# K in channel halves, bf16 masks, and dh's product on two engines, in a training step of a state-space layer with a gated feed-forward

## The chip, the core and the metric

The kernel runs on one core of one Trainium2 chip. The core has TensorE for matrix products (they land in PSUM), VectorE, ScalarE and GpSimd for elementwise work, and SyncE, which here only issues DMAs; ScalarE and GpSimd issue DMAs too. Each engine carries out its own instructions in order and waits for the others by semaphores. In the profile's rows the engines are called PE, PEld (TensorE's weight loads), DVE (VectorE), ACT (ScalarE), POOL (GpSimd) and SP (SyncE); a q behind the name is the engine's queue of DMA issues. The metric is the device time of one execution in microseconds (us).

## The reference

The layer is `out = x + s * g` on x of 2048 positions by 512 channels (bf16), and the kernel returns it together with the gradients for the eleven inputs of which it is a function, given `grad_out`. With xn the layer norm of x:

```python
# s: diagonal state-space layer (512 channels, 128 states), as a causal convolution
P = exp(dt*A[:, :, None] * arange(L));  K = einsum("dn,dnl,dn->dl", C, P, dt*B).real
y = irfft(rfft(pad(xn)) * rfft(pad(K)))[:L];  s = y + xn * Dskip
# g: feed-forward with silu on both sides, 1792 hidden units
h = silu(xn @ w1);  g = silu(h @ w2)
out = x + s * g
# _out, _vjp = jax.vjp(f, A_u, A_re, A_im, B_re, B_im, C_re, C_im, log_dt, Dskip, w1, w2); return out, *_vjp(grad_out)
```

Positions l are rounded to bf16 in the reference (`arange(L)` is cast to the type of A), so beyond 256 several lags share one value of K: 656 rows of K (some of them padding) stand for the 2048 lags.

## The kernel before

**Tiling.** Positions lie on the 128 partitions, 16 to a partition; so a tile of x, xn, DS or DO is 128 x 16 x 512 in bf16. The convolution is done as a Fourier transformation in two steps: a product with a 128-point table (TF, TI) over the partitions and 16-point products (Wf, Vi) with a 32 x 32 transposition on VectorE between them (`turn`, the STREAM_TRANSPOSE rows). It runs for one half H of the channels at a time, 256 of 512. `fwd_first` is the first step (eight groups, each evicted from PSUM into FA), `fwd_second` the second; `inv_first` and `inv_mm` are the way back. `cplx_mul` multiplies two spectra on VectorE.

**Stages.** Stage 1 (to about 158 us) computes the layer norm, the feed-forward forward pass, the powers of the state-space eigenvalues and, in `gen_masks`, small constants, among them MK, a mask with the lag values (float32). Stage 2 makes K: for four chunks of channels, `chunk_tables` builds tables X and CY on VectorE, `chunk_K` multiplies them into Kout (four steps for a chunk, called k in the score; chunk b and half u of it hold channels 32b + 16u to 32b + 16u + 15 of each of four blocks of 128), and `gen_xt` transposes X, collects it in XT (four buffers) and stores it (t). The spectra of xn (u) run beside it, then those of DS (f), the gradient that reaches y. At the end of the stage `store_K` writes all of Kout to the DRAM tile Kud; `load_K`, early in stage 3, reads it back as K_b with the rows repeated for the 2048 lags, by 17 DMAs on the queues of SP, ScalarE and GpSimd. `K_b` takes the place that DO_all has later.

Stage 3 transforms K (a, b: `forward` for half 0 and 1), multiplies spectra (p, e; and d, `chain`, for the gradient of K), goes back for y (x) and for the gradient of xn (z), turns each result into output: S_s and DO_all (y, `YOut.out`, after `YOut.sil` and `YOut.pre`, s), DXC (c), dK (v). `sums` (g) adds the lags that share a row of K and stores them in dKgd; `early` (t of the third score) loads them into Gt.

Stage 5 holds four things beside each other: the gradient of w2 (w, `Dw2`), the slabs of the state-space gradients (l, `Slabs`: `Gb` spreads Gt by the mask MK into Gbd, `P2` multiplies Gbd with XTl, `D3` and `P3` finish; y is `gen_y`, the other operand), the gradient of h (h, `Bwd.dh`), and after it the gradients of xn (x, `Bwd.dx`), of w1 (m) and the final output (z, `Out0`). A step of `dh` takes two tiles of 128 hidden units for 512 positions, computes silu' on ScalarE (sd), multiplies on TensorE into PSUM (ps_da), multiplies both on VectorE into dhT (line 1740), and turns the step before, through dhk, into DRAM (dhd).

**Order.** The order of the work is written out by hand as strings, the scores: `play` takes one letter after the other and runs the next piece of the generator with that name. A capital letter lets the piece evict PSUM on VectorE (`ev`, line 77, and `evs`), a small one on ScalarE. Pieces that only issue a DMA can be held (`hold`, `flush`) until the next piece of their kind. Nothing else orders the work: each engine and each DMA queue takes what it was given, in that order.

```python
nc.vector.tensor_tensor(out=self.dhT[:, f0:f0 + 2, :], in0=ps[:], in1=sd[:], op=ALU.mult)   # dh
MK = const.tile([P, 2, 16, 2], F32, name="MK")                                              # gen_masks
```

Of the kernel before, what the change touches and what calls it, by code (L numbers as in the profile page):

```python
# [138 lines left out]

def fwd_first(k, A, src, H):  # L140

    nc = k.nc
    d = slice(HW * H, HW * H + HW)
    for q in range(8):
        ps = k.pd.tile([P, 2, 2, HW], F32, name="ps_f", tag="pd")
        for j in range(2):
            for c in range(2):
                nc.tensor.matmul(out=ps[:, j, c], lhsT=k.TF[:, 2 * q + j, c, :], rhs=src(2 * q + j)[:, d], start=True, stop=True)
# [68 lines left out]
def kernel(ctx, tc, A_u, A_A_re, A_A_im, A_B_re, A_B_im, A_C_re, A_C_im, A_log_dt, A_Dskip, B_x, B_w1, B_w2, grad_out,  # L217
# [50 lines left out]
def gen_masks(k):  # L268
# [656 lines left out]
def chunk_K(k, b, t):  # L925
# [4 lines left out]
    for u in range(2):  # L930
# [1021 lines left out]
```

## Time and profile before

| what | us |
|---|---|
| median of 3 runs (679.77 to 685.35) | 682.53 |
| profiled execution | 682.6 |
| its span, first to last instruction | 680.8 |
| TensorE busy | 571.8 |
| VectorE busy | 570.1 |
| ScalarE busy | 453.6 |
| GpSimd busy | 96.0 |

The page gives an engine's busy time, its share of the span and its instructions; a matmul's end is modelled, and products overlap, so a busy TensorE is not one at its peak. The mean granted TensorE clock was 0.953. In rows of groups, `out<-in` are the program's names, then the shape, the count, the busy time in us and the mean of one in ns, and behind the second bar the idle time ahead of them with what ended it. In rows of waits stand the waiting engine, tile and line, what it waited for, the total in us, the number of waits and the longest. In rows by stretch stand its ends and length, then busy time and instruction count of PE, PEld, DVE, ACT and POOL, the granted clock, the share of the DMA engines and GB/s.

### The profile page before, as it was taken

The page shows a single profiled execution, that of the slowest core. Times are in us where ns is not written, and L with a number is a line of the kernel's source. Part 1 is how long each engine was busy: PE and PEld are TensorE (multiplying, and loading weights), DVE is VectorE, ACT ScalarE, POOL GpSimd, SP SyncE. Part 2 cuts the span into 40 slices and gives each one's busy share as a digit, 9 for nine tenths or more (in the row PEclk, how much of TensorE's full clock was granted, in tenths as well). Part 3 has the DMA queues.
Part 4 walks back from the last instruction along what each step waited for, and adds up shares of the span by engine and source line. Part 5 has one row for each costly group of instructions (what it writes and reads, how often), then busy time and mean ns, then how long its engine had stood idle before and what let it go on. Part 6 is the DMA issues. An engine that isn't in the chain of part 4 may idle for free. (4 is left out here: it accounts for less than half of the span.)

```text
span 680.8 us, 14322 instructions
## 1 busy us (share of the span) xinstructions
PE 571.8 (84%) x5668; PEld 339.3 (50%) x5668; DVE 570.1 (84%) x940; ACT 453.6 (67%) x551; POOL 96.0 (14%) x170
## 2 busy tenths in 40 slices
PE   2798877886777787779897869799998898999997
PEld 1344333334666576557675645355544544544553
DVE  5899978859899847888989997968998997879655
ACT  4799988967689955898979943465546645343341
POOL 1121100020100314211212251122201000000000
PEclk9989988977798997899999979799999999999999
DMA  8756568573899879965467879879978948986976
GB/s 252 233 182 222 198 219 283 195 241 146 248 278 300 257 199 258 324 224 166 134 194 238 201 196 255 232 187 257 254 204 209 250 135 254 266 245 196 315 228 204
DMA packets 173622, 154.58 MB, mean 227 GB/s; under 512 B 70574, under 2 KB 141750, under 8 KB 173556
## 3 DMA queue, kind: packets, MB, share of 16 engines
q1 hardware_dynamic: 157428, 112.70, 57.5%
q0 software_dynamic: 11920, 38.08, 17.3%
q10 hardware_dynamic: 4208, 2.89, 1.5%
q8 instruction: 44, 0.72, 0.4%
q14 instruction: 22, 0.18, 0.1%
HBM read 76.81 MB, written 67.65 MB: 212 GB/s over the span
## 5 line engine op out<-in xcount | busy, mean ns | idle before, releaser
L723 PE MATMUL ps_h<-XNT,W 128*128 128x512 bf16 x224 | 59.7, 418 | 20.7 <-ACT hs L77 14.4
L696 PE MATMUL ps_o<-W,aT 128*128 128x512 bf16 x224 | 55.3, 397 | 3.1 <-ACT aT L725 3.1
L1739 PE MATMUL ps_da<-DOT,W2T 128*128 128x512 bf16 x224 | 52.8, 379 | 1.1 <-DMA dhd<-dhk 0.9
L1568 PE MATMUL ps_w<-DO_all,KXW 128*128 128x512 bf16 x224 | 53.2, 391 | 0.0
L1801 PE MATMUL ps_dx<-KXW,dhT 128*128 128x512 bf16 x224 | 51.3, 379 | 1.4 <-DVE dhk L77 1.4
L723 PEld LDWEIGHTS <-W 128*128 128x128 bf16 x224 | 23.3, 105 | 52.8 <-issue 31.6
L1901 PE MATMUL ps_w<-dhc,xn 128*128 128x448 bf16 x256 | 49.2, 353 | 0.0
L77 ACT CAST FZ<-ps_i 128x1024 bf16<-128x1024 f32 x44 | 43.1, 1034 | 4.6 <-PE ps_i L187 4.6
L77 ACT CAST FA<-ps_f 128x1024 bf16<-128x1024 f32 x39 | 38.4, 1048 | 10.4 <-PE pt_xt L1012 7.4
L1740 DVE TENSOR_TENSOR dhT<-ps_da,sd 128x1024 bf16<-128x1024 f32 x28 | 34.1, 1221 | 13.2 <-ACT sd L213 12.3
L173 PE MATMUL ps_s<-FA,Wf 128*64 128x256 bf16 x384 | 35.0, 318 | 10.9 <-ACT FX L77 6.8
L1810 ACT ACTIVATE dxn<-dxn,c,rstd 128x512 f32<-128x512 f32 x16 | 13.0, 814 | 44.2 <-DVE c L1809 44.2
L696 PEld LDWEIGHTS <-aT 128*128 128x128 bf16 x224 | 22.7, 102 | 33.0 <-issue 5.3
L77 ACT CAST Vb<-ps_V 128x1024 bf16<-128x1024 f32 x26 | 26.0, 1016 | 19.1 <-PE ps_V L1637 14.7
L77 ACT COPY dhk<-pt_dh 128x1024 bf16<-128x1024 bf16 x20 | 20.1, 1007 | 27.0 <-DMA dhd<-dhk 17.8
L77 ACT COPY XT<-pt_xt 128x1024 bf16<-128x1024 bf16 (+1 forms) x35 | 32.5, 967 | 8.1 <-PE pt_xt L1012 3.1
L1901 PEld LDWEIGHTS <-xn 128*128 128x128 bf16 x256 | 25.0, 98 | 23.7
L187 PEld LDWEIGHTS <-Vi 64*128 64x128 bf16 x576 | 27.4, 95 | 16.9 <-issue 6.5
L1568 PEld LDWEIGHTS <-KXW 128*128 128x128 bf16 x224 | 21.4, 100 | 26.7 <-issue 5.4
L1360 PE MATMUL ps_v<-FZ,TI 128*128 128x256 bf16 x192 | 25.2, 282 | 10.9 <-DVE FZ L162 8.5
L1801 PEld LDWEIGHTS <-dhT 128*128 128x128 bf16 x224 | 21.3, 98 | 25.4 <-issue 2.3
L1739 PEld LDWEIGHTS <-W2T 128*128 128x128 bf16 x224 | 21.2, 98 | 25.3 <-issue 2.2
(313 smaller groups left out, 1457.1 us busy)
## 6 DMA issues: line engine op xcount, KB each, us to landing
XTd<-XT SPq DMA_DIRECT2D x20, 512.0 KB, 4.6
XP<-UXd POOLq DMA_DIRECT2D x16, 512.0 KB, 4.9
XTl<-XTd SPq DMA_DIRECT2D x31, 256.0 KB, 4.8
hTd<-hs SPq DMA_DIRECT2D x28, 256.0 KB, 3.4
aTd<-aT SPq DMA_DIRECT2D x28, 256.0 KB, 2.8
dhc<-dhd SPq DMA_DIRECT2D x16, 448.0 KB, 6.1
XYd<-XYg SPq DMA_DIRECT2D x25, 256.0 KB, 3.8
hsb<-hTd SPq DMA_DIRECT2D x18, 256.0 KB, 3.1
```

Of the source, the lines that this page charges most:

```text
L77: (k.nc.vector.tensor_copy if k.by_dve else k.nc.scalar.copy)(out=out, in_=in_)
L173: nc.tensor.matmul(out=ps[64 * h:64 * h + 64, c, j], lhsT=k.Wf[:, c, 0:64], rhs=A[:, 2 * (v + j) + h], start=True, stop=True)
L187: nc.tensor.matmul(out=ps[:, h, j], lhsT=Vc[z], rhs=y[z, c, v % 4 + j, :], start=(n == 0), stop=(n == len(Y) - 1))
L696: nc.tensor.matmul(out=pso[:], lhsT=aT[:, ft, tt * P:(tt + 1) * P], rhs=W2[:, ft, :], start=(ft == 0), stop=(ft == FT - 1))
L723: nc.tensor.matmul(out=ps[:, j], lhsT=W1[:, dk, ft * P:(ft + 1) * P], rhs=XNT[:, dk], start=(dk == 0), stop=(dk == DK - 1))
L1360: k.nc.tensor.matmul(out=ps[:, j], lhsT=k.TI[:, t0 + j, c, :], rhs=Z[:, 2 * (t0 + j) + c], start=(c == 0), stop=(c == 1))
L1568: nc.tensor.matmul(out=ps[:], lhsT=A[:, t, :], rhs=k.DO[:, t, :], start=(t == 0), stop=(t == T - 1))
L1739: nc.tensor.matmul(out=ps[:, j], lhsT=self.W2T[:, ft // 2, dk, j * P:(j + 1) * P], rhs=self.DOT[tc_][:, dk], start=(dk == 0), stop=(dk == ...
L1740: nc.vector.tensor_tensor(out=self.dhT[:, f0:f0 + 2, :], in0=ps[:], in1=sd[:], op=ALU.mult)
L1801: nc.tensor.matmul(out=psx[:], lhsT=dhT[:, ft, t % 4 * P:(t % 4 + 1) * P], rhs=self.W1T[:, ft, :], start=(ft == 0), stop=(ft == FT - 1))
L1810: nc.scalar.activation(out=dxn[:], in_=dxn[:], func=ACT.Identity, scale=k.rstd[:, t:t + 1], bias=c12[:, 0:1])
L1901: nc.tensor.matmul(out=ps[:], lhsT=k.xn[:, t, dk * P:(dk + 1) * P], rhs=ch[i][:, t, :], start=(t == 0), stop=(t == T - 1))
```

## The change

- **Halves.** H no longer means the lower or upper 256 channels but every second block of 64 (`half`): half 0 holds the channels 128x to 128x + 63, which are complete when chunks 0 and 1 of K are done. `store_K` writes one half after chunk 1 and one after chunk 3, from within `chunk_K`, to a DRAM tile of its own; `load_K` reads one half, called by a new part h (`taps`), once in stage 2 and once in stage 3; and half 0's first transformation, a, may begin in the second score of stage 3. K_b's halves lie in `dkp`, a pool now opened in stage 2, and in the place of DO. XT gets three buffers instead of four.
- **Layout behind it.** xn, DS, DO and DXC are now read or written in blocks of 64 channels. `YOut` loads co and cG as two full rows of 512 channels for a partition, multiplies them into DO_all early (`pre`), and `out` multiplies the convolution into DO_all in place. dKgd is split by halves, and Gt is loaded by 20 DMAs instead of 6. Out0's first product is made for each position by itself, into g.
- **Masks.** MK is bf16 and holds each value twice, and Gbd is laid out so that the innermost step of every operand is one element. The weights of `P2` are then 32 columns with a step of 16 elements.
- **dh.** ScalarE copies ps_da to dhT as bf16, and VectorE multiplies that in place with sd.
- **Places.** T12 of the slabs and two of the last stage's big tiles lie in `dkp`.
- **Orders.** All scores are new.

```diff
-SCORE_1 = "pppppppppppppggpgpppGppgppppgppppgppppppgppppppgppgppgpppgppppggppppppppgppppgpMpgpppGpgpppppppgpgppppggpmpmmppppgppppgpppppgpppppppppgmgppmmpMgggGmmgttGmgmggmmmgGgggGmttGgt"
+SCORE_1 = "ppppppppppppppppggggGpgpppppgpppgppppgpgppppppppppgppppppgppppgpgppppgppppggpppppMGpppgppppgpppppggpppppGpppmgmpppgppgpppppggpgpppppmpgpppgmGgpmpGgmMmmggpgmGgmmmtggttGtGmmtg"
 SCORE_2 = (
-    "guTuuuuuuuuwttTtgUtKttkkgctgtttkggtotgtuuuttkTtgucttgktgtkgtkto",
-    "uT",
-    "uuuuutuKkuguuwukwtkctwgUugwuuggtutuutTuKtKTKk",
-    "ttT",
+    "",
+    "uuguwuwuttuTTtTKugkuttkttcktuougggugugut",
+    "ttuutuuttTgcktkkgtgtutkgotuuuttguwhuuKUtkcgtggtttuuguutktktuutwwUtt",
+    "KKTKk",
 )
 SCORE_3 = (
-    "Tt",
-    "UFqFqFqkFFFffttqftfffqFnknuffDffffkfUfTuUDfffddFdn",
-    "kaaFadafdafdndkfdkDsdFdfaffafBvvDvAbbvidaddskbkgsabgagaFgdddGddDapijDpabdasadaixbxbvevjxtvvzjxtisgzpBjigpxgeggxtxzeizesxzzjbzzijiXfzbbyybbsepbpbsycsbxxcxpyxxpzxgsxxzejxezcljzqsylsesssyzyzzslYZZCsCCCC",
+    "TTu",
+    "ffffnfffqfAhafqaaqakTqfkfFfffuqnfFTDUuUffffTkffffdadnadFdtfddFkfdkfd",
+    "dFkdfDffbbabdbvDvkvvddjgaadagnddgFsdaegiddkGifaabDqiddbaabppabdxitxvtxjvpxvxvBxzzejzbgipjsessxzexiXzigszsggsgistbbpbbpbszzpbjgsszybxysxjspsjxexxjeexxexxssylyzczzzzzzzZylycccyclcCCY",
 )
 SCORE_5 = (
-    "wuuuyuuwlWWywwhYlwLYllYylywylyllwwullwlhhwlhlwL",
-    "YLlHlWwYulyLhylwhyllwlwwYhwLyYYLwwlhylwlwyWLHwwlWloYlhHlolLhyloLoooloyhllYxlllLhxLlxlxxlx",
-    "xzxxHzhhzxxhhxHfHxfxxxhxHxhxthftHtthxxxhzxxxfhxtmtttzfftfxxftmtmtMxftmmfffxMxxttfftfzmMfzzfmffmrtrrmrzz",
+    "luwWhuhLyWuwwywuyyLwywHwLlhYulWlwLlyuhlWlwulylHlw",
+    "yYYLhYLyLwlHWywlHlWlwYWwLllyWYHwllylwWHlwlLwwHoollylloyloLhyylolYoloHlllhLLyxLxLllxxxl",
+    "xzxxHxhzhxxHhfxfHthxxxxHxhxxfHHHtthxxtxxfhzxxhxtxtxtfMfffttmtfmtxtmfMftfMztffMfxtzxfxtmzmMmzrzffftzrrzmr",
 )
+def half(x, H):
+    return x.rearrange("p (x h r) -> p x h r", h=2, r=64)[:, :, H] if len(x.shape) == 2 else x.rearrange("p t (x h r) -> p t x h r", h=2, r=64)[:, :, :, H]
...
-                nc.tensor.matmul(out=ps[:, j, c], lhsT=k.TF[:, 2 * q + j, c, :], rhs=src(2 * q + j)[:, d], start=True, stop=True)
+                nc.tensor.matmul(out=by64(ps[:, j, c]), lhsT=k.TF[:, 2 * q + j, c, :], rhs=src(2 * q + j, H), start=True, stop=True)
...
-    MK = const.tile([P, 2, 16, 2], F32, name="MK")
+    MK = const.tile([P, 2, 16, 2, 2], BF16, name="MK")
...
+        if end and u:
+            store_K(k, b // 2)
         yield
-def store_K(k):
+def store_K(k, H):
     for e in range(2):
         for s in range(2):
             z = 32 * (2 * e + s) + e
-            d0 = 256 * e + 128 * s
-            (k.nc.scalar if s else k.nc.sync).dma_start(k.Kud[:, d0:d0 + 128].rearrange("(h l) d -> l h d", l=16), k.Kout[z:z + 32 - e:2])
+            d0 = 128 * e + 64 * s
+            (k.nc.scalar if s else k.nc.sync).dma_start(k.Kud[H][:, d0:d0 + 64].rearrange("(h l) d -> l h d", l=16), k.Kout[z:z + 32 - e:2, :, 64 * H:64 * H + 64])
...
-            XT = xs.tile([P, 8, 2, P], BF16, name="XT", tag="XT", bufs=4)
+            XT = xs.tile([P, 8, 2, P], BF16, name="XT", tag="XT", bufs=3)
...
+    def taps():
+        K_b = k.K_b = [k.dkp.tile([P, T, HW], BF16, name="K_b", tag="dK")]
+        for H in range(2):
+            if H:
+                K_b.append(k.do.tile([P, T, D], BF16, name="K_b", tag="DO")[:].rearrange("p t d -> p (t d)")[:, 0:T * HW].rearrange("p (t d) -> p t d", d=HW))
+            load_K(k, K_b, H)
+            yield
...
         for H in range(2):
-            d = slice(HW * H, HW * H + HW)
-            g = k.dKgd[0:640, d].rearrange("(h l) d -> h l d", l=16)
-            nc.sync.dma_start(Gt[2 * H::4], g[0:32])
-            nc.sync.dma_start(Gt[1 + 4 * H:62 + 4 * H:8], g[32:40])
-            nc.sync.dma_start(Gt[65 + 4 * H:66 + 4 * H, 0, :], k.dKgd[640:641, d])
+            for e in range(2):
+                g = k.dKgd[H][0:640, 128 * e:128 * e + 128].rearrange("(h l) (s r) -> h l s r", l=16, s=2)
+                for s in range(2):
+                    nc.sync.dma_start(Gv[2 * e::4, :, s, H], g[0:32, :, s])
+                    nc.sync.dma_start(Gv[1 + 4 * e:62 + 4 * e:8, :, s, H], g[32:40, :, s])
+                nc.sync.dma_start(Gv[65 + 4 * e:66 + 4 * e, 0, :, H], k.dKgd[H][640:641, 128 * e:128 * e + 128].rearrange("a (s r) -> a s r", s=2))
...
-            r[nm] = k.y2.tile([P, 4, HW], BF16, name=nm, tag=nm, bufs=3)
-            q.dma_start(r[nm][:], piece(src, n))
+            r[nm] = k.y2.tile([P, 2, D], BF16, name=nm, tag=nm, bufs=3)
+            q.dma_start(r[nm][:], src[:, 2 * n:2 * n + 2, :])
...
-        TT(out=S[:], in0=S[:], in1=g[:], op=ALU.mult)
-        TT(out=S[:], in0=S[:], in1=x[:], op=ALU.add)
+        for t in range(TS):
+            gx = g[:, t].rearrange("p (x h r) -> p x h r", h=2, r=64)
+            TT(out=gx, in0=S[:, t].rearrange("p (h x r) -> p x h r", h=2, r=64), in1=gx, op=ALU.mult)
+        TT(out=g[:], in0=g[:], in1=x[:], op=ALU.add)
...
-        self.G[i] = self.sw.tile([P, 16, 2, 16, 2], BF16, name="Gbd", tag="Gbd", bufs=2)
+        self.G[i] = self.sw.tile([P, 2, 16, 2, 8, 2], BF16, name="Gbd", tag="Gbd", bufs=2)
...
+        src = k.Gt[:, :, c0:c0 + 16].unsqueeze(2).to_broadcast([P, 16, 2, 16])
         for g2 in range(2):
-            nc.vector.tensor_tensor(out=G[:, :, g2], in0=k.Gt[:, :, c0:c0 + 16].rearrange("p l g -> p g l").unsqueeze(3).to_broadcast([P, 16, 16, 2]),
-                                    in1=k.MK[:, g2].unsqueeze(1).to_broadcast([P, 16, 16, 2]), op=ALU.mult)
+            nc.vector.tensor_tensor(out=G[:, g2].rearrange("p l e n m -> p l e (n m)"), in0=src, in1=k.MK[:, g2].rearrange("p l e m -> p (l e) m").unsqueeze(2).to_broadcast([P, 32, 8, 2]), op=ALU.mult)
...
-        nc.vector.tensor_tensor(out=self.dhT[:, f0:f0 + 2, :], in0=ps[:], in1=sd[:], op=ALU.mult)
+        d = self.dhT[:, f0:f0 + 2, :]
+        nc.scalar.copy(out=d, in_=ps[:])
+        nc.vector.tensor_tensor(out=d, in0=d, in1=sd[:], op=ALU.mult)
```

More of the change, by code (lines that the diff above doesn't have):

```diff
@@ L922, in chunk_tables, with chunk_K @@
     yield
-def chunk_K(k, b, t):
+def chunk_K(k, b, t, end):
     nc = k.nc
@@ L1235, in forward @@
             yield
+    play(k, SCORE_3[0], **parts)
+    drain(k, parts, "w")
+    banks(k, 3, 1)
+    assert k.turned >= 33
+    lo.close("w2s", "xc", "ko", "sa", "mm")
+    ro.close("cyb")
+    k.do = lo.open("do"); k.mm = lo.open("mm", 3); k.fa = lo.open("fa", 2)
+    k.ux = lo.open("ux", 6)
+    k.sel = lo.open("sel")
+    k.row = k.sel.tile([DK, P], BF16, name="row")
+    sels = []
+    FA, W1 = (k.fa, "FA"), (k.tfp, "W1")
+    parts.update(a=forward(0, *FA), q=skip(), n=gsum_sel(k, k.sel, sels), k=loads(Uk, k.UXd), d=chain())
+    play(k, SCORE_3[1], **parts)
+    drain(k, parts, "tu")
+    ro.close("sb", "xs", "uw")
+    k.kxw = ro.open("kx").tile([P, 8192], BF16, name="KXW", tag="KX")
+    dkp = k.dkp
+    k.y2 = ro.open("y2", 2)
+    y = k.y = YOut(k)
+    for n in range(3):
+        y.load(n)
     def products(Y, U, conj):
@@ L1257, in gates @@
             yield
+            if n == 0:
+                assert got.count(0) and got.count(1)
+                k.DO = k.do.tile([P, T, D], BF16, name="DO_all", tag="DO")
             y.pre(n)
```

123 lines of the change are left out of this document (51 added, 72 removed).

## The prediction

> **What bounds the kernel now.** I read the page's busy times first, then busy time by stage, then the waits of the stages that leave most room, then the groups that the change touches.
>
> ```profile
> span 680.8 us, 14322 instructions
> PE 571.8 (84%) x5668; PEld 339.3 (50%) x5668; DVE 570.1 (84%) x940; ACT 453.6 (67%) x551; POOL 96.0 (14%) x170
> PE 17%; DMA 9%; DVE 8%; ACT 3%; issue 2%; SPq 1%; DVEq 0%; ACTq 0%
> 407.76 9.19 DMA XYy<-XYd
> ```
>
> No engine is full over the span, and the chain that ended last has no owner: followed back it reaches only to 407.76 us, and of these 40% of the span TensorE holds 17, DMA 9 and VectorE 8. So the room must be looked for stage by stage. The next rows give, after the stretch and its length, the busy time of TensorE, its weight loads, VectorE, ScalarE and GpSimd.
>
> ```profile
> 158.00:246.00 88.00, 65.05 (x1478) 52.16 (x1481) 78.50 (x132) 72.06 (x84) 11.61 (x20) 0.90 0.79 239
> 246.00:300.00 54.00, 41.92 (x535) 32.88 (x524) 40.87 (x52) 38.99 (x43) 14.19 (x30) 0.91 0.90 263
> 300.00:396.00 96.00, 85.29 (x1070) 64.03 (x1070) 91.35 (x74) 86.01 (x92) 20.09 (x32) 1.00 0.64 185
> 396.00:420.00 24.00, 17.98 (x124) 10.31 (x123) 18.64 (x21) 5.37 (x7) 9.92 (x15) 0.86 0.90 241
> 448.00:520.00 72.00, 70.17 (x696) 37.69 (x698) 61.94 (x87) 40.43 (x47) 12.98 (x25) 1.00 0.86 226
> 420.00:620.00 200.00, 185.69 (x1639) 97.29 (x1637) 171.90 (x275) 105.74 (x119) 22.43 (x42) 0.98 0.83 223
> ```
>
> Two stretches are badly filled: 246 to 300 us, where the busiest engine works 41.92 of 54 us, and 396 to 420 us, where it works 18.64 of 24. Between them VectorE is the bound (91.35 of 96, 95%). Behind them TensorE is (185.69 of 200, 93%; 97% between 448 and 520), with VectorE at 86% and ScalarE at 53%. The change touches all four.
>
> **Part A, K by halves.** Here is the hole it aims at, as waits between 246 and 300 us and as the accesses to K.
>
> ```profile
> ACT FA L77 <- PE pt_xt L1012: 7.4, 1, 7.4
> DVE XT L77 <- ACT Kout L77: 4.2, 1, 4.2
> DVE FX L77 <- PE ps_s L173: 2.6, 3, 1.9
> PE pt_xt L1012 <- ACT XT L77: 3.3, 1, 3.3
> L956 ACTq DMA_DIRECT2D Kud<-Kout x2: 663/676/690, 248.1 to 248.8; - x2
> L956 SPq DMA_DIRECT2D Kud<-Kout x2: 712/1100/1489, 249.1 to 249.9; - x2
> L977 ACTq DMA_DIRECT2D K_b<-Kud x1: 348/348/348, 257.1 to 257.1; - x1
> L980 ACTq DMA_DIRECT2D K_b<-Kud x1: 1265/1265/1265, 257.5 to 257.5; - x1
> L983 ACTq DMA_DIRECT2D K_b<-Kud x1: 1341/1341/1341, 258.8 to 258.8; - x1
> L148 PE MATMUL ps_f<-K_b,TF x64: 269/273/284, 284.7 to 334.7; 128*128 128x256 bf16 x64
> ```
>
> K is stored at 248 to 250 us and its loads are issued from 257.1 on: they follow the stores' landing. ScalarE issues three of them, and it is in order: its evictions stand behind DMA issues that cannot go yet, which is the idle 7.4 us, whatever name the wait carries. K is first read at 284.7, so K itself is not waited for; what is lost is the blocked queue, and the fact that only the spectrum of DS and the lag chain are there to interleave, each a series of product, eviction and transposition. After the change, half 0 is stored with the eighth of 16 steps of K, and eleven score entries lie between that and its loads; half 1 has fourteen between store and load. The block should go, and one whole forward transformation of K (eight evictions, one turn) becomes filler for this stretch. Were it filled as well as the stretch behind it, it would take 41.92 / 0.95 = 44 us: at most 10 gained. Of the other side: two more stores and three more loads are issued by ScalarE, 2 x 0.676 + 0.348 + 1.265 + 1.341 = 4.3 us if none is covered. I take -6, nearer to the full hole, since the filler is real work that stands at 284 to 300 us today. **A: -6, between -10 and +4.3.**
>
> The layout goes with it and I cost it at nothing: products, evictions and the DO multiplications keep count and size, with runs of 64 elements in them. If the 16 multiplications of DO lost their pace through that and ran like the 1213 ns rows below rather than at 684, it would be 16 x 0.53 = 8.5 us on VectorE; the rows show no such pattern, so this stays as an upper end.
>
> ```profile
> L1326 SPq DMA_DIRECT2D Gt<-dKgd x2: 546/572/599, 336.8 to 353.5; - x2
> L1327 SPq DMA_DIRECT2D Gt<-dKgd x2: 601/620/639, 337.5 to 354.1; - x2
> L1328 SPq DMA_DIRECT2D Gt<-dKgd x2: 383/394/406, 338.2 to 354.8; - x2
> L1624 DVE TENSOR_TENSOR Gbd<-Gt,MK 128x512 bf16<-128x512 bf16 x32 | 20.4, 682 | 0.0
> DMA packets 173622, 154.58 MB, mean 227 GB/s; under 512 B 70574, under 2 KB 141750, under 8 KB 173556
> q1 hardware_dynamic: 157428, 112.70, 57.5%
> ```
>
> Gt's loads become 20 instead of 6, on SP: at these durations 2 x (4 x 0.57 + 4 x 0.62 + 2 x 0.39) = 11 us of SP's queue instead of 3. Gt is loaded by 355 us and first read by L1624 after 411 us, so some 50 us cover it. Pieces shrink: counted from the access patterns, K's stores go from 256 to 128 bytes (4 x 16 x 41 = 2,624 pieces become 5,248), K's loads from some 1,024 pieces of 2 KB to 2,048 of 1 KB, Gt's from 2 x (32 x 16 + 8 x 16 + 1) = 1,282 of 512 bytes to 5,128 of 128; against that, co and cG are read in runs of 2 KB instead of 512 bytes, 16 x 128 x 4 = 8,192 pieces becoming 2,048. The net is some 1,350 packets on 173,622. By the q1 row a packet takes 0.575 x 16 x 680.8 us / 157,428 = 40 ns of one engine, so the 6,470 added pieces of 128 bytes are 16 us of all sixteen engines, spread over 100 us.
>
> [...] No row here separates the rate of a 128-byte piece from that of a 512-byte one.
>
> **Part B, the seam at 396 to 420 us.**
>
> ```profile
> PE ps_v L1360 <- DVE FZ L162: 6.0, 1, 6.0
> ACT Y L1035 <- DMA XYy<-XYd: 18.6, 1, 18.6
> ```
>
> TensorE waits 6.0 us for the last transposition, with nothing but products of its result ahead in the order; ScalarE waits 18.6 us for a load. In the new order the last turn of x (Z) is followed by outputs of y, a step of l and evictions that do not need it, and stage 5 plays h, dh's first steps, at its fifth entry instead of its fifteenth. The 6.0 is the ceiling, zero the floor, if SP or GpSimd deliver XTl no sooner. **B: -3.**
>
> **Part C, fewer evictions on VectorE in stage 3.** Capital letters evict on VectorE: F falls from 11 to 6, D from 6 to 4, C from 5 to 2.
>
> ```profile
> L77 DVE CAST FA<-ps_f 128x1024 bf16<-128x1024 f32 x9 | 10.5, 1213 | 0.4 <-PE ps_f L148 0.4
> L77 ACT CAST FA<-ps_f 128x1024 bf16<-128x1024 f32 x39 | 38.4, 1048 | 10.4 <-PE pt_xt L1012 7.4 <-PE ps_f L148 2.9
> ```
>
> Ten go: 12.1 us off VectorE, 10.5 onto ScalarE. From 300 to 396 the two hold 91.35 and 86.01; level, at 88.7 and the same 95%, the stretch would take 93 instead of 96. **C: -2, between -3 and 0.**
>
> **Part D, stage 5.**
>
> ```profile
> L1740 DVE TENSOR_TENSOR dhT<-ps_da,sd 128x1024 bf16<-128x1024 f32 x28 | 34.1, 1221 | 13.2 <-ACT sd L213 12.3 <-PE ps_da L1739 0.7
> L1462 DVE TENSOR_TENSOR zS<-zS,zg 128x1024 bf16<-128x1024 bf16 x8 | 5.5, 684 | 9.3 <-DMA zg<-gd 9.3
> L901 DVE TENSOR_TENSOR m<-X 128x512 bf16<-128x512 bf16 x4 | 1.7, 414 | 0.0
> L213 ACT ACTIVATE sd<-hsb 128x1024 bf16<-128x1024 bf16 x28 | 29.3, 1057 | 0.0
> L77 ACT COPY dhk<-pt_dh 128x1024 bf16<-128x1024 bf16 x20 | 20.1, 1007 | 27.0 <-DMA dhd<-dhk 17.8 <-PE pt_dh L1755 7.3 <-issue 1.1
> L77 DVE COPY dhk<-pt_dh 128x1024 bf16<-128x1024 bf16 x8 | 5.5, 684 | 4.8 <-DMA dhd<-dhk 4.8
> L1637 PEld LDWEIGHTS <-Gbd 128*32 128x32 bf16 x512 | 11.9, 97 | 9.3 <-issue 4.2 <-DVE T L1652 1.4 <-DVE Gbd L1624 0.4
> ```
>
> dh's product on VectorE falls from 1221 to the 684 of an all-bf16 product of the same size: 28 x 0.54 = 15 us off. The mask product falls from 682 to the 414 of a bf16 product of 512: 32 x 0.27 = 8.6 off. Out0 splits one product in two: 8 x (2 x 0.414 - 0.684) = 1.2 on. More capitals (H 8 to 15, W, M) put back about 6. VectorE: -16. ScalarE takes 28 copies like L77's at 1.05, 29 us, and loses some 8: +21 on 105.74 of 200, 63% then. TensorE remains the bound; at the 97% of 448 to 520 its 185.69 would take 191, so 9 is the ceiling. Of what could cost: the new copy is queued on ScalarE behind sd and behind dhk's eviction, which waits 17.8 us in all for its buffer's store; behind the copy stand the PSUM slot that ps_da shares with ps_V, and so TensorE. Today the product waits 12.3 us for sd on the same queue, so the block is not new, and H in capitals takes dhk off ScalarE. Weight loads for L1637 now step over 32 bytes; they run beside the products, so I cost them at nothing, with 9 us (512 x 18 ns, up to the 115 of a larger load) if bare. **D: -4, between -9 and +24** (half of the 28 copies and half of the 17.8 bare).
>
> **Part E, order in stages 1 and 2, and three XT buffers for four.**
>
> ```profile
> XTd<-XT SPq DMA_DIRECT2D x20, 512.0 KB, 4.6
> ```
>
> No work changes in stage 1. In 158 to 246, VectorE's 78.5 of 88 leaves 5 us to gain; one XT store late costs 4.6. **E: +1, between -5 and +5.**
>
> **Sum.** -6 - 3 - 2 - 4 + 1 = -14. The profiled execution took 682.6 us (680.8 and 1.8 around it), beside a median of 682.53: 668.6, rounded to 668.5.
>
> **The rivals.**
> 1. Full relief. Everything reaches its ceiling but E: 682.6 - 10 - 6 - 3 - 9 = 655. For it: VectorE and ScalarE each lose a block that others wait for. Against: an order rarely fills every gap.
> 2. It doesn't do what it says: the halves are ready early, but the work that they feed is bound by VectorE later (300 to 396 is at 95%), so the hole only moves; the seam moves too. Only D's and C's halves remain: 682.6 - 2 - 1 + 1 = 680.5.
> 3. Slower: ScalarE gates dh. Where an eviction of dhk waits for its store, the copy behind it holds a PSUM slot, and TensorE stops. It decides once ScalarE's step (sd 1.06, copy 1.05, Vb 1.02, dhk 1.01, with the wait) is longer than TensorE's work between two dh. With A and B kept: 682.6 - 9 - 2 + 1 + 24 = 696.5.
> 4. Small pieces: the added packets' 16 us all fall on waits for K or Gt: 684.5. [...]
>
> **How the numbers follow.** Forecast 0.42, rival 1 0.15, rival 2 0.20, rival 3 0.17, rival 4 0.06. A measurement of this kernel tells about 1% (6.8 us) from nothing. Faster by more: forecast and rival 1, and a little of rival 2, 0.60; slower by more: rival 3 and the upper half of rival 4, 0.20; the rest 0.20. The range reaches from rival 1 to the lower part of rival 3; below 654 and above 694 I leave about 0.1 each: 654 to 694.
>
> **What would show it.** A: no idle of 7 us on ScalarE after K's stores, ps_f from K before DS's spectrum ends, and 246 to 300 shrunk by 6. B: PE's wait for FZ under 2. D: L1740's successor at 0.68, L1624 at 0.41, and the copy without a wait behind it. Wrong it would be if TensorE waited for the copy of ps_da, if ScalarE still stood behind K's loads, or if Gt came after TensorE asked for it.

## The result, and the profile after

The changed kernel takes 690.26 us (median of 9 runs, 685.29 to 692.33); 9 runs of the kernel before beside them gave 682.11. The ratio is 1.0101 (95%: 1.0068 to 1.0134): it is slower by 1%, where 668.5, 2% faster, was forecast. The range, 654 to 694, holds it. The profiled execution took 688.8 us (before: 682.6).

The page of the changed kernel, to be read against the first rows of the prediction:

```profile
span 687.0 us, 14390 instructions
PE 571.3 (83%) x5668; PEld 344.2 (50%) x5668; DVE 544.5 (79%) x950; ACT 480.0 (70%) x577; POOL 101.5 (15%) x181
DMA packets 179175, 154.59 MB, mean 225 GB/s; under 512 B 78846, under 2 KB 147174, under 8 KB 179108
q1 hardware_dynamic: 161108, 112.70, 57.6%
```

The work did change as forecast: VectorE lost 25.6 us, ScalarE got 26.4, TensorE kept its 571. The span grew by 6.2 all the same. The groups that carry it, from the same page and from the view of groups:

```profile
L1767 DVE TENSOR_TENSOR dhT<-dhT,sd 128x1024 bf16<-128x1024 bf16 x28 | 19.3, 691 | 34.0 <-ACT dhT L1766 33.8
L1766 ACT CAST dhT<-ps_da 128x1024 bf16<-128x1024 f32 x28 | 28.2, 1006 | 15.6 <-PE ps_da L1764 15.1
L1650 DVE TENSOR_TENSOR Gbd<-Gt,MK 128x512 bf16<-128x512 bf16 x32 | 12.0, 418 | 0.0
L1662 PEld LDWEIGHTS <-Gbd 128*32 128x32 bf16 x512 | 15.1, 143 | 11.7 <-issue 4.7 <-DVE Gbd L1650 4.5 <-DVE YTl L77 0.4
```

dh's product fell from 1221 to 691 ns and the mask's from 682 to 418. But the product stands idle for 33.8 us behind ScalarE's copy, where 12.3 us behind sd were lost before.

Next the same stretches as in the prediction (stretch, length, then PE, PEld, DVE, ACT, POOL busy, granted clock, DMA share, GB/s):

```profile
158.00:246.00 88.00, 65.63 (x1490) 55.03 (x1494) 69.53 (x120) 67.58 (x76) 18.12 (x28) 0.83 0.77 220
246.00:300.00 54.00, 43.61 (x552) 32.67 (x544) 40.35 (x49) 47.34 (x52) 14.98 (x30) 1.00 0.80 238
300.00:396.00 96.00, 86.46 (x1074) 67.01 (x1071) 90.11 (x76) 86.97 (x93) 17.68 (x32) 0.98 0.67 192
396.00:420.00 24.00, 16.31 (x93) 7.05 (x94) 6.80 (x11) 4.09 (x4) 10.32 (x17) 0.79 0.75 212
420.00:620.00 200.00, 182.16 (x1576) 96.86 (x1575) 152.97 (x277) 120.45 (x133) 21.76 (x39) 0.97 0.82 214
```

246 to 300 is filled better (ScalarE 47.34 for 38.99). 396 to 420 is emptier: VectorE works 6.80 us there (18.64 before), and TensorE's granted clock is 0.79 (0.86 before). In the kernel before, though, stage 3 still ran in the first 16 of these 24 us.

Where the time went is seen best by milestones. They are starts (first) and ends (last) of instructions on the timelines of the two kernels; the last column is the changed kernel's lead:

| milestone | before | after | lead |
|---|---|---|---|
| first ps_f of xn (stage 2's spectra) | 161.3 | 149.7 | 11.6 |
| last eviction of Kout (K complete) | 247.7 | 247.4 | 0.3 |
| first / last ps_f of K_b | 284.7 / 334.9 | 257.5 / 326.0 | 27.2 / 8.9 |
| last DXC (stage 3 ends) | 411.9 | 396.4 | 15.5 |
| first ps_w (w2's gradient) | 410.0 | 399.8 | 10.2 |
| last ps_w of w2's gradient | 512.9 | 516.7 | -3.8 |
| last ps_V | 543.7 | 550.6 | -6.9 |
| last ps_dx | 648.5 | 653.4 | -4.9 |

So the kernel gains twice and loses twice: 11.6 us are won in stage 1 and gone by the end of stage 2; 15.5 us are won in stage 3 and are gone by the last product of w2's gradient, some 120 us later. The first rows of that seam, as waits between 396 and 420 us:

```profile
POOL XTl L1639 <- ACT XTl L1616: 29.0, 1, 29.0
DVE dhT L1767 <- ACT dhT L1766: 8.7, 1, 8.7
PE ps_da L1764 <- DMA W2T<-W2Td: 4.8, 1, 4.8
ACT Vb L77 <- PE ps_V L1662: 4.6, 1, 4.6
POOL XTl L1639 <- PE ps_V L1662: 5.5, 1, 5.5
POOL hsb L1749 <- ACT sd L225: 4.2, 1, 4.2
```

and the accesses to two tiles that stage 5 loads first, XTl and XYy, in the changed kernel:

```profile
L1616 ACT ACTIVATE XTl<-lvf x1: 1087/1087/1087, 394.2 to 394.2; 128x1024 f32<-128x1024 f32 x1
L1045 POOL DMA_DIRECT2D XYy<-XYd x4: 933/968/997, 418.1 to 476.1; - x4
```

and in the kernel before:

```profile
L1591 ACT ACTIVATE XTl<-lvf x1: 1107/1107/1107, 397.3 to 397.3; 128x1024 f32<-128x1024 f32 x1
L1030 POOL DMA_DIRECT2D XYy<-XYd x4: 943/961/1001, 407.8 to 476.1; - x4
```

Stage 5 begins with a fill of XTl's first buffer on ScalarE. GpSimd's loads are queued behind it, and GpSimd stood 29.0 us for it (5.8 before). The fill is only 3.1 us earlier than before, though stage 3 ends 15.5 us earlier, since ScalarE now makes six of DXC's eight evictions (three before), the last at 393.3. XYy is asked for 10.3 us later than before, though the fill is done at 395.3: in the new order it stands on GpSimd's queue behind two more issues, which waited 4.2 us for sd and 5.5 us for ps_V. This became the theory to test: the lead is lost because stage 5's first loads didn't move with it. The rival was VectorE's wait for ScalarE's copy.

### The profile page after: what moved, and what is told of

The parts are those of the page before. It is cut to its first block, busy times and chain, and to the rows that moved or that the text cites. A ratio compares the mean times of both kernels' runs of the same rounds, so it can differ in the third digit from the quotient of the medians.

```text
span 687.0 us, 14390 instructions
## 1 busy us (share of the span) xinstructions
PE 571.3 (83%) x5668; PEld 344.2 (50%) x5668; DVE 544.5 (79%) x950; ACT 480.0 (70%) x577; POOL 101.5 (15%) x181
## 2 busy tenths in 40 slices
DMA packets 179175, 154.59 MB, mean 225 GB/s; under 512 B 78846, under 2 KB 147174, under 8 KB 179108
## 3 DMA queue, kind: packets, MB, share of 16 engines
q1 hardware_dynamic: 161108, 112.70, 57.6%
## 5 line engine op out<-in xcount | busy, mean ns | idle before, releaser
L735 PE MATMUL ps_h<-XNT,W 128*128 128x512 bf16 x224 | 55.4, 393 | 13.6 <-ACT hs L77 10.5
L1764 PE MATMUL ps_da<-DOT,W2T 128*128 128x512 bf16 x224 | 55.0, 390 | 5.5 <-DMA W2T<-W2Td 4.8
L708 PE MATMUL ps_o<-W,aT 128*128 128x512 bf16 x224 | 52.7, 384 | 0.0
L77 ACT CAST FZ<-ps_i 128x1024 bf16<-128x1024 f32 x47 | 46.8, 1070 | 4.2 <-PE ps_i L199 4.2
L77 ACT CAST FA<-ps_f 128x1024 bf16<-128x1024 f32 x47 | 46.1, 1056 | 2.2 <-PE ps_f L160 2.2
L1767 DVE TENSOR_TENSOR dhT<-dhT,sd 128x1024 bf16<-128x1024 bf16 x28 | 19.3, 691 | 34.0 <-ACT dhT L1766 33.8
L77 ACT CAST Vb<-ps_V 128x1024 bf16<-128x1024 f32 x23 | 23.2, 1016 | 26.5 <-PE ps_V L1662 26.2
L1766 ACT CAST dhT<-ps_da 128x1024 bf16<-128x1024 f32 x28 | 28.2, 1006 | 15.6 <-PE ps_da L1764 15.1
L708 PEld LDWEIGHTS <-aT 128*128 128x128 bf16 x224 | 22.2, 99 | 27.4 <-issue 1.8
L185 PEld LDWEIGHTS <-Wf 128*64 128x64 bf16 x384 | 23.4, 118 | 24.6 <-issue 18.5
L77 ACT CAST FX<-ps_s 128x1024 bf16<-128x1024 f32 x27 | 26.7, 1026 | 11.5 <-DMA UXd<-FX 6.3
```

What stands on the lines that cost most here:

```text
L77: (k.nc.vector.tensor_copy if k.by_dve else k.nc.scalar.copy)(out=out, in_=in_)
L185: nc.tensor.matmul(out=ps[64 * h:64 * h + 64, c, j], lhsT=k.Wf[:, c, 0:64], rhs=A[:, 2 * (v + j) + h], start=True, stop=True)
L708: nc.tensor.matmul(out=pso[:], lhsT=aT[:, ft, tt * P:(tt + 1) * P], rhs=W2[:, ft, :], start=(ft == 0), stop=(ft == FT - 1))
L735: nc.tensor.matmul(out=ps[:, j], lhsT=W1[:, dk, ft * P:(ft + 1) * P], rhs=XNT[:, dk], start=(dk == 0), stop=(dk == DK - 1))
L1764: nc.tensor.matmul(out=ps[:, j], lhsT=self.W2T[:, ft // 2, dk, j * P:(j + 1) * P], rhs=self.DOT[tc_][:, dk], start=(dk == 0), stop=(dk == ...
L1766: nc.scalar.copy(out=d, in_=ps[:])
```

## The experiments

All ratios are to the kernel before, run on the same chip, with 95% intervals; 0.1% is 0.7 us.

### The order of stage 5

**e1**: the changed kernel with the old SCORE_5.

```diff
 SCORE_5 = (
-    "luwWhuhLyWuwwywuyyLwywHwLlhYulWlwLlyuhlWlwulylHlw",
+    "wuuuyuuwlWWywwhYlwLYllYylywylyllwwullwlhhwlhlwL",
...
```

> The changed kernel with the stage-5 score of before, nothing else. Theory (the loss is the new order at the start of stage 5; the other parts brought stage 5 forward by 10 to 15 us and lighten VectorE): 672 to 677, the lead of about 13 us at 395 us kept to the end. Rival (ScalarE gates dh through its copy, in any order): 686 or more, as the change.

Measured: 683.92 us, 1.0036 (1.0013 to 1.0059). The new order of stage 5 costs 0.65%, 4.4 us (2.7 to either side); but the lead isn't kept either. Its waits between 394 and 450 us:

```profile
ACT Y L1050 <- DMA XYy<-XYd: 20.4, 1, 20.4
PE pt_do L1742 <- ACT KXW L77: 10.7, 1, 10.7
```

Stage 3's end was 397.7, XYy's load was issued at 407.6, and behind ScalarE's 20.4-us wait for it stood the eviction on which TensorE waited 10.7. Both theories had missed: the order is part of the loss, and the longest wait left on ScalarE is for a load.

**e2**: the changed kernel with y's first step, which asks for XYy, at the front of its SCORE_5.

```diff
-    "luwWhuhLyWuwwywuyyLwywHwLlhYulWlwLlyuhlWlwulylHlw",
+    "yluwWhuhLWuwwywuyyLwywHwLlhYulWlwLlyuhlWlwulylHlw",
```

> The changed kernel with the first y of stage 5 moved from ninth to first letter, so that XYy's load is issued before any load that waits on GpSimd's queue. Theory (order at the start): XYy's load issued near 405 instead of 418.1, the first multiplication of Y 5 to 10 us earlier, 682 to 686 in all. If the wait for W2T and the transposing DMAs on SP is what counts instead: 688 to 691. Rival (ScalarE gates dh): 690.

Measured: 698.72 us, 1.0249 (1.0218 to 1.0280), far above all three expectations. XYy was asked for at 406.6 instead of 418.1, as expected, and yet:

```profile
DVE dhT L1767 <- ACT dhT L1766: 28.2, 2, 24.6
ACT Y L1050 <- DMA XYy<-XYd: 27.4, 1, 27.4
PE ps_da L1764 <- ACT DOT L1743: 20.8, 1, 20.8
```

The step also copies XYy on ScalarE. That copy now stood first in ScalarE's order and held everything behind it for 27.4 us. A letter moves an issue and a wait together; only the issue must go ahead.

### The first loads of stage 5

**e5**, **e6**, **e8**: XYy's first load is issued when the slabs are set up, on GpSimd, ahead of everything else there, and the fill is a memset on GpSimd. e5 is e1 with this, e6 the changed kernel, e8 the kernel before. The load and the fill move together in all three, so their shares aren't told apart.

```diff
-        k.nc.scalar.activation(out=self.flat(0), in_=k.lvf[:, 0:1].to_broadcast([P, 1024]), func=ACT.Copy, scale=0.0)
+        self.y0 = sw.tile([P, 7, 2, 64, 2], BF16, name="XYy", tag="XYy", bufs=1)
+        k.nc.gpsimd.dma_start(self.y0[:].rearrange("p i c q e -> p i (c q e)"), k.XYd[:, 17:24, 0])
+        k.nc.gpsimd.memset(self.flat(0), 0.0)
...
-    load(0)
+    ld[0] = S.y0
```

> The changed kernel with before's order of stage 5 (as in e1), and with the first loads of stage 5 taken off ScalarE: the fill of XTl's first buffer is a memset on GpSimd, and the load of XYy for the first quarter is issued ahead of it. Theory 'the lead is lost at the start of stage 5, because its loads are issued by GpSimd only behind ScalarE's fill, which stands behind ScalarE's last evictions': XYy is issued some 10 us earlier than e1's 407.6, ScalarE's 20.4-us wait for it falls under 12, TensorE's 10.7-us wait for ScalarE at pt_do falls under 3, and the time goes from 683.9 to between 674 and 678. Rival 'whatever is won at 400 to 420 is waited for later, since from 420 on the order is bound by something else (VectorE, DMA)': those two waits shrink, and the time stays between 681 and 685. Rival 'the memory of these buffers is free only then': XYy is issued as late as before, and nothing moves.

> The changed kernel with its own order of stage 5 and the same two edits of the loads. Here XYy was issued at 418.1 behind loads that wait for sd and for ps_V, and ScalarE's copy of Y, VectorE's m and TensorE's pt_yt waited 7.6, 7.6 and 4.6 us. Theory 'loads at the start of stage 5': these three waits go, TensorE's 4.8-us wait for W2T (SP's queue) stays, and the time is 3 to 7 us less than the change's: 683 to 687. Rival 'the new order of stage 5 loses its time later, between 450 and 550, by VectorE's waits for ScalarE's copy of ps_da': 688 to 691.

> The kernel before with the two edits of the loads alone. A control: there stage 3's last evictions end at 410.7, and the loads issued from 397 on run beside them. Theory 'the loads are late only where stage 3 ends early': within 2 us of before, 680 to 684. Rival 'the loads cost every version their wait (ScalarE waits 18.6 us for XYy in before too)': 674 to 678.

| | late loads | early loads | gain |
|---|---|---|---|
| changed kernel, its order (e6) | 1.0101 | 1.0020 (0.9990 to 1.0049), 682.68 us | 0.81% = 5.5 us (3.0 to either side) |
| changed kernel, old SCORE_5 (e1, e5) | 1.0036 | 0.9979 (0.9950 to 1.0007), 680.15 us | 0.57% = 3.9 us (2.5 to either side) |
| kernel before (e8) | 1 | 1.0036 (1.0008 to 1.0064), 683.01 us | -0.36% = -2.5 us (1.9 to either side) |

In e6 XYy is asked for at 380.3, 38 us sooner, and the copy of Y no longer waits for it; the first loads of XTl go out only 2 us sooner, at 393.7; TensorE's wait for W2T, on SP's queue, stays, as expected:

```profile
L1617 POOL DMA_DIRECT2D XYy<-XYd x1: 956/956/956, 380.3 to 380.3; - x1
```

```profile
DVE dhT L1769 <- ACT dhT L1768: 14.6, 3, 8.7
PE ps_da L1766 <- DMA W2T<-W2Td: 4.7, 1, 4.7
```

The control, e8, tells what kind of effect it is: the same edit doesn't make the kernel before faster. Its waits between 394 and 420 us:

```profile
ACT KXW L77 <- PE ps_w L1568: 16.1, 1, 16.1
ACT Y L1035 <- DMA XYy<-XYd: 1.2, 1, 1.2
```

ScalarE's wait for XYy fell from 18.6 to 1.2 us, and it now stands 16.1 us for the first products of w2's gradient, which come behind stage 3's last ones. This fits a load that was covered there by stage 3's tail, and became a cost where that tail got shorter. Why e8 is slower isn't shown; in its profiled execution, the longest of its ten, TensorE's wait for FZ grew from 6.0 to 8.4 us and stage 3 ended at 417.2 instead of 411.9. e6's gain lies within the 3 to 7 us of its theory. e5 stands at 680.15 where 674 to 678 were expected, so late loads are a part of the lost lead, not the whole.

### The split of dh's product, and the masks

**e3**: the kernel before with the bf16 masks and the split; **e10**: with the masks alone.

```diff
-        nc.vector.tensor_tensor(out=self.dhT[:, f0:f0 + 2, :], in0=ps[:], in1=sd[:], op=ALU.mult)
+        d = self.dhT[:, f0:f0 + 2, :]
+        nc.scalar.copy(out=d, in_=ps[:])
+        nc.vector.tensor_tensor(out=d, in0=d, in1=sd[:], op=ALU.mult)
...
-    MK = const.tile([P, 2, 16, 2], F32, name="MK")
+    MK = const.tile([P, 2, 16, 2, 2], BF16, name="MK")
```

> The kernel before, its orders, with bf16 masks and with dh's product split, nothing else. Theory (the arithmetic is good or harmless): 676 to 682. Rival (the copy on ScalarE gates dh): 688 to 697, with TensorE waiting for the copy of ps_da.

> The kernel before with the bf16 masks and the new layout of Gbd alone (VectorE's product for Gbd 418 ns in place of 682, 32 times, about 8 us less of VectorE). With e3 (masks and split, 687.4 against 682.0) it tells the two parts of D apart. Theory 'the split costs, the masks are neutral': 679 to 683. Rival 'the new layout of Gbd costs TensorE or moves a wait': 684 to 688, and the split is neutral.

e3: 687.4 us, 1.0081 (1.0051 to 1.0112). e10: 682.44 us, 1.0006 (0.9984 to 1.0027). The masks are neutral (1.5 us to either side) though they take 8.4 us off VectorE; the split costs 0.75%, 5.1 us (2.5 to either side). e3 itself lies above its theory and just below its rival's 688. Between 450 and 650 us e3's product waits as the changed kernel's does:

```profile
DVE dhT L1742 <- ACT dhT L1741: 35.1, 21, 4.0
```

**e4**: the changed kernel without the split (the first three lines of the diff above turned back); **e7**: e5 without it.

> The changed kernel with dh's product back on VectorE alone. Theory (order at the start of stage 5): 688 to 693, no gain. Rival (ScalarE gates dh): 676 to 683.

> e5 with dh's product on VectorE alone, as before the change (1221 ns out of PSUM, no copy on ScalarE). If the split is worth what VectorE loses by it (0.5 us x 28, of which a part is on the path), e5 is 2 to 6 us faster than this kernel; if ScalarE's copy ahead of VectorE's product is a wait that costs what it saves, as e3 against before suggests (5 us slower with the split and the bf16 masks), this kernel is 2 to 5 us faster than e5: 670 to 676 where e5 stands at 674 to 678.

e4: 691.67 us, 1.0149 (1.0120 to 1.0177). e7: 675.05 us, 0.9904 (0.9871 to 0.9937). So the price of the split hangs on the order around it. Under the old order of stage 5, twice, it costs 0.75%. In the changed kernel's own order, which was laid out with it, taking it away makes things 0.5% slower, 3.3 us, just clear of noise (2.9 to either side). **e7 is faster than both kernels**, by 1.0% and, from the two ratios, 2.0%: halves, masks and the new orders up to stage 3, with the old order of stage 5, early loads and no split.

**e13**: e5 with VectorE's product issued one step later, so that the copy is long done; **e17**: TensorE's transposition of the finished block one step later as well.

```diff
         nc.scalar.copy(out=d, in_=ps[:])
-        nc.vector.tensor_tensor(out=d, in0=d, in1=sd[:], op=ALU.mult)
+        self.late.append((d, sd))
+        self.mul(2 if n % 7 == 6 else len(self.late) - 1)
...
-        if n:
-            self.turn(n - 1)
+        if n > 1:
+            self.turn(n - 2)
```

> e5 (before's order of stage 5, early loads, dh's product split) with VectorE's product of a step issued behind the next step's matmuls and ScalarE's next copy, not behind its own copy; the last two steps of a quarter are done together. In e5 that product waits for the copy 29.0 us in 19 waits between 450 and 650, and e5 is 5.1 us slower than e7, which has no split. Theory 'the split costs because VectorE stands, in order, at the product until ScalarE's copy is done': the waits fall under 12 us and the time goes from 680 to between 674 and 677. Rival 'the split costs because of the 28 us of copies on ScalarE, in front of its other evictions': the waits fall as well, and the time stays at 678 to 682.

> e13 (split, product one step later) with TensorE's transposes of a finished dh block moved one step later as well, so that TensorE doesn't stand at pt_dh for a product that VectorE has yet to reach (13.5 us in 6 waits in e13's 420 to 560). Theory 'the split costs by in-order waits alone, on VectorE in e5 and on TensorE in e13': both waits are gone, 674 to 678, e7's time or better. Rival 'the split costs by the 28 copies on ScalarE, which are in front of its other evictions (DVE's T waited 20.5 us for Vb in e13, 12.8 in e5)': 680 to 695, with T's wait for Vb as long as in e13 and no wait of TensorE for dhT.

e13: 702.23 us, 1.0326 (1.0260 to 1.0391), far off both expectations. Its waits between 420 and 560 us:

```profile
DVE T L1676 <- ACT Vb L77: 20.5, 7, 7.2
PE pt_dh L1793 <- DVE dhT L1784: 13.5, 6, 3.6
```

VectorE's wait for the copy has fallen to 1.5 us here. In its place TensorE, in order, waits 13.5 us at the transposition for a product that VectorE reaches only after its slab work (21.8 us over the whole run, against 2.9 in e5). e17 takes that away: 678.24 us, 0.9954 (0.9924 to 0.9985). Its rows between 420 and 660 us, and then e5's:

```profile
DVE T L1676 <- ACT Vb L77: 19.3, 7, 7.0
DVE dhT L1784 <- ACT dhT L1768: 8.3, 7, 3.1
```

```profile
DVE dhT L1769 <- ACT dhT L1768: 35.3, 22, 4.0
DVE T L1676 <- ACT Vb L77: 12.8, 7, 6.5
```

The wait for the copy fell from 35.3 to 8.3 us, TensorE doesn't wait for dhT, and of the 0.75% about a third came back by the ratios, with intervals of e5 and e17 that overlap; so neither expectation is borne out. What makes up the rest isn't settled. VectorE's wait for Vb, behind ScalarE's copies, is 12.8 us in e5, 14.0 in e7 and 19.3 in e17, so it doesn't sort the three by their time.

### The first order

**e12**: e7 with the old SCORE_1.

```diff
-SCORE_1 = "ppppppppppppppppggggGpgpppppgpppgppppgpgppppppppppgppppppgppppgpgppppgppppggpppppMGpppgppppgpppppggpppppGpppmgmpppgppgpppppggpgpppppmpgpppgmGgpmpGgmMmmggpgmGgmmmtggttGtGmmtg"
+SCORE_1 = "pppppppppppppggpgpppGppgppppgppppgppppppgppppppgppgppgpppgppppggppppppppgppppgpMpgpppGpgpppppppgpgppppggpmpmmppppgppppgpppppgpppppppppgmgppmmpMgggGmmgttGmgmggmmmgGgggGmttGgt"
```

> e7 with before's order of stage 1. The changed kernel's xn spectrum starts at 149.7 us in place of 161.3, and its last eviction of Kout is at 246.7, as late as before's 247.0. Theory 'the 11 us won in stage 1 are lost again in stage 2, which is bound by its own waits (ScalarE's FX for a store of 6.3 us, TensorE's for FX and TF of 10.6 and 9.2)': Kout's last eviction stays within 3 us of 247 and the time within 3 us of e7's 675. Rival 'stage 2 runs as long whenever it begins': Kout's end and the whole move by 8 to 11 us, 683 to 686.

Measured: 683.07 us, 1.0012 (0.9979 to 1.0044): 1.08%, 7.4 us, slower than e7. Kout was complete at 253.7 instead of 246.6 and stage 3 ended at 404.9 instead of 395.8. The rival was right, in the main: of 10 us of lead into stage 2, 7 leave it. So the changed stage 2 takes some 7 us longer than the old one did, and stage 1's new order pays for it. No run tells stage 2's new order apart from what came with it, the three XT buffers and K's stores and loads in its midst. From Kout's end to stage 3's end, however, e12 needs 151.2 us, the changed kernel 149.0 and the kernel before 164.2.

### What the start of stage 5 still loses

e7's lead at stage 3's end is 16.1 us, and 7.7 of it reach its profiled end (673.1 against 680.8). Its busy time at the seam, and two of its waits between 394 and 450 us:

```profile
410.00:420.00 10.00, 4.45 (x32) 2.12 (x33) 1.58 (x3) 2.42 (x3) 0.51 (x1) 0.59 1.06 216
```

```profile
ACT KXW L77 <- DMA out_dram<-KXW: 16.4, 1, 16.4
PE ps_w L1593 <- DMA KXW<-aTd: 5.1, 1, 5.1
```

**e9**: e7 with the store of a block of w2's gradient ahead of the next transposing load on SP's queue. **e14**: e7 with four of the first five loads of W2T moved to later letters.

```diff
+        nc.sync.dma_start(self.o[:, ft, :], ob)
         if ft + 3 < FT:
             self.load(ft + 3)
-        nc.sync.dma_start(self.o[:, ft, :], ob)
```

```diff
-    "wuuuyuuwlWWywwhYlwLYllYylywylyllwwullwlhhwlhlwL",
+    "wyuwlWWywwhYlwuLYlluYylyuwylylulwwlluwlhhwlhlwL",
```

> e7 with one pair of lines swapped: the store of a finished block of w2's gradient is issued on SP's queue before the transposing load of the block after next, not behind it. In e7 that store was issued at 412.7, behind a load that held SP for 8.5 us, and ScalarE's next eviction of ps_w waited 16.4 us for it (400.4 to 416.8), with Vb's eviction and DOT's copy queued behind; TensorE did 4.5 us of work in 410 to 420. Theory 'what the start of stage 5 still loses in e7 is SP's queue, in order': the store goes out at about 404, the 16.4-us wait falls under 8, and the time goes from 675 to between 668 and 672. Rival 'the wait passes to the transposed load itself' (TensorE waited 5.1 us for KXW in e7): 673 to 677, with a longer wait of TensorE for KXW.

> e7 with the loads of W2T (256 KB each) spread over the first part of stage 5: one of the first five stays near the start, four come later, each still ahead of the step of dh that reads it (the first at about 440). Theory 'what the start of stage 5 still loses is the transfers themselves: in e7 the DMA share is 1.06 in 410 to 420, so a store issued 8 us sooner (e9) landed no sooner': with 1 MB less to move in 396 to 420, ScalarE's 16.4-us wait for the store and TensorE's 5.1-us wait for KXW shrink, and the time goes from 675 to between 669 and 673. Rival 'what is taken out there is missing later, or the transposed loads set the pace whatever runs beside them': 674 to 678.

e9: 677.84 us, 0.9933 (0.9905 to 0.9961). The store went out at 404.9, 7.8 us sooner, and ScalarE's wait for it fell from 16.4 to 12.7 only; TensorE's wait for the transposed load stayed at 5.2. e14: 679.05 us, 0.9956 (0.9921 to 0.9990), no better either, and ScalarE's wait for the store grew. That wait, between 394 and 450 us, and SP's queue (start, us, engine, line):

```profile
ACT KXW L77 <- DMA out_dram<-KXW: 22.1, 1, 22.1
```

```profile
401.34 6.88 SPq L1586 DMA_TRANSPOSE KXW<-aTd  x1
408.31 0.53 SPq L1600 DMA_DIRECT2D out_dram<-KXW  x1
408.95 0.60 SPq L1641 DMA_DIRECT2D XTl<-XTd  x1
409.64 13.44 SPq L1586 DMA_TRANSPOSE KXW<-aTd  x1
```

With four W2T loads out of the way, the next transposing load came sooner (409.6 instead of 413.9) and held SP for 13.4 us (3.2 in e7), beside the XTl loads. Both theories on e7's rest are refuted. The rivals don't fit in full either: both times lie about 1 us above their ranges, and e9's longer wait of TensorE didn't come. That the transposing loads and XTl together set the pace there is the reading left; it isn't shown, nor that they can't be made faster.

**e15**, e13 and e14 in one:

> e13 with e14's order of the W2T loads: split, product one step later, W2T spread. If both theories hold their gains add: 668 to 673. If only the later product helps: 674 to 677; if neither does: 679 to 682.

Measured: 707.61 us, 1.0389 (1.0336 to 1.0443), far above all three expectations, with e13's loss in it. Neither helps, so nothing adds up.

## Why the prediction was wrong

The four parts of the change, from the ratios 1.0006 (masks), 1.0081 (with the split), 1.0036 (with halves and the orders of stages 1 to 3) and 1.0101 (with stage 5's order): 0.4, 5.1, -3.1 and 4.4 us, with about 1.5, 2.5, 2.6 and 2.7 us to either side, in this sequence. In another sequence they differ: with early loads stage 5's order costs 2.8 us, hardly clear of noise (e6 against e5). Old order and early loads together take 8.3 us off the changed kernel (e5), the product without the split another 5.1 (e7); e7 then has 6.5 of the 14 us that were forecast. The step that failed is the sum: it carried what stages 1 to 3 win through the seam at full size, and added a gain for D.

- **A was right.** ScalarE's block at K's loads is gone: half 0 is loaded at 216, K's products begin at 257.5. With e12's old stage 1, Kout ends 6.0 us later than before and K's last product 0.5 earlier, so 6.5 are won between them, some of it perhaps C's; 6 were forecast. From Kout's end to stage 3's end 13.0 us are won in e12 and 15.2 in the changed kernel. That stretch holds A, C and B's wait for FZ, 6.0 of which 2.2 are left; -6, -2 and B's ceiling of -6 make 14. So the gains up to stage 3's end had about the right size. **C** isn't measured by itself; thirteen of the evictions of FA, FX, FZ and DXC left VectorE between 246 us and stage 3's end, not ten.
- **E's sum was right, its parts not.** The orders of stages 1 and 2 together give 0.3 us at Kout's end, where +1 was forecast. But "No work changes in stage 1" passed over an order that starts the spectra 11.6 us sooner, worth 7.4 us at the end (e12), and stage 2 loses as much: among its waits between 158 and 247 us ScalarE's eviction FX stood 6.3 us for a store, and TensorE 10.6 us for FX. First the changed kernel's rows, then the row of the kernel before, where FX's wait for the store was 1.0 us in all:

```profile
PE ps_s L185 <- ACT FX L77: 10.6, 3, 5.4
ACT FX L77 <- DMA UXd<-FX: 6.3, 1, 6.3
```

```profile
PE ps_s L173 <- ACT FX L77: 6.3, 6, 2.5
```

- **B is the step that failed most.** It took the gap as what TensorE waits for FZ, 6.0 with zero as the floor. That wait fell to 2.2. But the sum adds the gains of A, C and E as if stage 5 began when stage 3 ends. It begins when its loads land, and these stand behind a fill on ScalarE and in the in-order queues of GpSimd and SP. I had quoted ScalarE's 18.6-us wait for XYy and put no price on it; e8 fits a load that the tail covered as long as the tail was there; and a floor of zero left no room for a loss. The 15.5-us lead shrank to 10.2 at the first product and to -3.8 at the end of w2's gradient. Early loads give 5.5 back (e6); stage 5's new order, which the prediction counted as a gain within B, costs 4.4 (e1). What takes the rest of the lead isn't settled.
- **D's sign hangs on the order.** -4 was forecast, between -9 and +24; in the old order the masks are worth nothing and the split costs 5.1. In the new order the split is worth 3.3 (e4), but that order costs 4.4 itself. The sizes were right (691 for 684 ns, 418 for 414; VectorE 25.6 us less in all). "TensorE remains the bound" fits e10, where 8.4 us less work on VectorE changed nothing. "The block is not new" was wrong: the product waited 12.3 us for sd, which is made ahead of the matmuls, and now 33.8 for a copy that can only start behind them. How that wait becomes time isn't settled (e13, e17).
- **The rivals.** Rival 3 had the right place, but not the cause of the result: without the split the changed kernel is slower still (e4), and its trace has no wait of TensorE for the copy of ps_da. That the range holds 690.26 was therefore luck: its upper end came from that wait. Rival 2 had the right shape, a gain that moves instead of staying, but stopped at 680.5. Rival 4 fell: K's products waited 0.3 us for its loads, and no product waited for Gt's. The packets rose by 5,553 and not 1,350, yet q1's time only from 0.575 x 680.8 = 391.5 to 0.576 x 687.0 = 395.7 us. Though 8,272 more packets lie under 512 B (78,846 for 70,574), a packet of q1 took 391.5 x 16 us / 157,428 = 39.8 ns of one engine before and 395.7 x 16 / 161,108 = 39.3 after, so the smaller pieces had no visible price here, as far as a mix of smaller and larger pieces can show it.

## What to carry to other kernels

A stage that ends sooner helps only if what the next one waits for is asked for sooner too: look for the instruction that releases its first loads, the queue it stands in, and what that queue does until then. Work that hides a load is part of the load's price; the same edit won 5.5 us in one kernel and lost 2.5 in the other. Handing half of an operation to another engine added a wait in two in-order queues: in the changed kernel the copy stood 15.1 us for ps_da and the product 33.8 us for the copy. In an order that wasn't laid out for it the split cost 5.1 us, and 8.4 us of relief for VectorE alone bought nothing.

## What was not expected of the hardware

**TensorE was slow behind the three pauses at the seam.** In the changed kernel, with the idle ahead in brackets:

```profile
398.90 0.92 PE L1662 MATMUL ps_V<-XTl,Gbd 128*32 128x256 bf16 x16 [3.11 <-DMA XTl<-XTd]
399.75 5.01 PE L1593 MATMUL ps_w<-DO_all,KXW 128*128 128x512 bf16 x16
410.44 3.59 PE L1764 MATMUL ps_da<-DOT,W2T 128*128 128x512 bf16 x8 [4.79 <-DMA W2T<-W2Td]
427.29 1.86 PE L1062 MATMUL pt_yt<-ident_bfloat,Y 128*128 128x128 bf16 x16 [4.63 <-DVE Y L897]
428.95 3.62 PE L1593 MATMUL ps_w<-DO_all,KXW 128*128 128x512 bf16 x8
437.16 1.89 PE L1593 MATMUL ps_w<-DO_all,KXW 128*128 128x512 bf16 x8
```

Eight products take 3.6 us after a pause and 1.89 in flow: 449 and 236 ns each. By such rows some 1.5 to 3 us more were lost behind each of the three pauses at the seam (3.1, 4.8 and 4.6 us), an estimate from the lengths of the products there. The granted clock was 0.71 from 398.9 to 404.8 us, behind the 3.1-us pause, where the sixteen products of ps_w took 313 ns each; it was 0.50 from 410.4 to 414.1 and from 427.3 to 432.6, behind the two longer ones, and 1.00 from 434.9 to 440.0, where they run in flow. What lowers it there isn't shown.

**A transposing load held its queue for 13.4 us** (e14), where the median of the fourteen is 2.9 in the changed kernel. Between 404 and 418 us of e14, with two of them on SP's queue, one behind the other, 115 GB/s were moved, where the changed kernel's mean is 225:

```profile
DMA packets 3000, 1.61 MB, mean 115 GB/s; under 512 B 2647, under 2 KB 2679, under 8 KB 3000
```

The XTl loads share this stretch, so it doesn't show what the transposing loads alone would move.

**The weight loads of Gbd, whose columns now lie 32 bytes apart, took 143 ns instead of 97** (L1662, L1637 before; 143 in e10 too, where only the masks and their layout changed), beyond the 115 that the prediction allowed. Before, the columns lay side by side. e10 takes as long as the kernel before (1.0006), so beside the products no price of theirs shows.
